# Other weights for spreading attention steps along the expert blocks

## The chip, the cores and the metric

The kernel runs on one core of one Trainium2 chip, as one launch. The metric is the device time in microseconds (us) of that launch. TensorE (PE) multiplies matrices, VectorE (DVE) and ScalarE (ACT) work on whole tiles, GpSimd (POOL) issues the indirect DMAs, SyncE (SP) issues the other DMAs.

## The reference

Two layers follow each other. The first is an attention over channels, for four batches of 5056 tokens by 256 channels. The second sends each of the 20224 token rows to one of eight experts, each with two matrices (256x1024 and 1024x256).

```python
qn = q / (norm(q, axis=1) + 1e-6); kn = k / (norm(k, axis=1) + 1e-6)
a  = softmax(kn.transpose(0, 2, 1) @ qn / tau)      # 256 x 256 in each batch
x  = (v @ a).reshape(B * N, 256)
e  = argmax(x @ w_gate, axis=1)                     # one expert for each row
out = gate_w * (relu(x @ w1[e]) @ w2[e])            # gate_w: the softmax weight of e
```

## The kernel before

**Side work and blocks.** A batch b has its attention cut into steps. For b = 2 and 3, 20 *chunks* of q and k give the scores (L205, L206); for b = 1 the scores come in the opening. 20 *norm* pieces give the column norms of the next batch (load L1268, square on ACT L1274). Then comes the *softmax*, and ten *groups* g = 0 to 9 of 512 tokens. A group takes: the values' scale (L1118, L1122), their two half-precision parts on ACT and DVE (L168, L175), four score products x t = 0 to 3 on PE (px, L1142), a copy of each from PSUM by ACT (xg, L1148), a square for the row's scale (xjunk, L1154), the choice of the expert on DVE (L388 to L412, r_m to r_ex), the *rank* products on PE (rtp, L417 and L420), the slots (L445, L448), the rows' two parts (L364 on ACT, L368 on DVE), and four scatters to DRAM by POOL (xs, L456).

The expert work is cut into 90 *blocks*: 72 of 256 rows and 18 of 128 rows, sorted by expert. A block n takes eight weight pieces that DVE copies out of the resident weights (wp, L629, five buffers), four first products on PE (hp, L640), a relu on ACT (L648) and the rest on DVE (ht, L651), four second products (y, L664), a scaling on ACT (o, L678) and two stores by POOL (out, L682). A first or a second product is a string of 12 matmuls. Strings of first products of block n and of second products of block n-1 alternate on PE.

**Stages.** A block can be loaded only when its rows have been scattered. Eleven places in the list of groups, ENDS, close a stage: (0,5), (0,9), and (b,2), (b,6), (b,9) for b = 1, 2, 3. After the rank of such a group a *table* is made: one product (ctp, L515) and some 27 small DVE operations (L518 to L578), from which the blocks of the next stage are known.

**The order.** PE, ACT, DVE and SP have their whole order written by a planner (lay, task). Each task has an engine, a guessed cost, what it depends on, and a due time; of the tasks that could start first on an engine the one with the earliest due time is taken. POOL takes its DMAs as they come. Once the order is made it is fixed: at run time an engine that waits holds all that is queued behind it.

**Due times of side work.** The list of side work, from group (0,8) on, is laid along the blocks: each entry has a weight, `amount` is the sum of the weights ahead of it, and an outline (hull) over the points (first block of a stage less two, amount at the stage's end) turns an amount into a block number. So an entry's due time follows from the weights alone, and the space that an entry gets is its weight's share. PE takes 10.48 us for a block of 256 rows with nothing else (1036.7 to 1047.2 in the trace).

Of the kernel before, what the change touches and what calls it, by code (L numbers as in the profile page):

```python
# [21 lines left out]
B, N, C = 4, 5056, 256  # L22
# [7 lines left out]
T = 4  # L30
# [4 lines left out]
ENDS = [(0, CUT - 1), (0, G - 1)] + [(b, g) for b in range(1, B) for g in (2, 6, G - 1)]  # L35
# [33 lines left out]
def attention_then_experts(ctx, tc, qk, qkc, vT, wts_in, kc, out):  # L69
# [33 lines left out]
    def halves(i):  # L103
        up = i % 2 == 0
        e = i // 2 if up else E - 1 - i // 2
        return e, ((2 * e, 2 * e + 1) if up else (2 * e + 1, 2 * e))
# [846 lines left out]
    for i in range(E):  # L953
        for k in range(2):
            task(("gram", i, k), pe, 0.93, [(("w", i, k), 1)] + ([("most", i - 1)] if i else []), call(w_gram, i, k), 5)
            n = halves(i)[1][k]
# [22 lines left out]
    for b in range(B):  # L979
        side = []  # L980
        if b == 1:
            side += [(("norm", b, n), 0.0, 0.6) for n in range(20)]
        if b > 1:
            side += [(("chunk", b, ch), 1.31, 1.2) for ch in range(NCH)]
        if b:
            side += [(("soft", b), 3.0, 7.0)]
        for g in range(AHEAD if b == 0 else 0, G):
            side += [(("x", b, g, t), 0.68 if b else 0.89, 1.9 if b else 1.2) for t in range(T)] + [(("rank", b, g), 0.3, 0.5)]
        for what, cost, weight in side:
            amount[what] = total  # L990
            total += weight
            done_by.append(total)
            spent.append(spent[-1] + cost)
            if what[0] == "rank" and what[1:] in ENDS[1:]:
                bounds.append(total)
# [473 lines left out]
```

## Time and profile before

| what | value |
|---|---|
| median of 3 runs | 1175.9 us (1173.66 to 1176.03) |
| the profiled execution | 1175.05 us |
| its span, first to last instruction | 1173.3 us |
| PE idle before 130 us (the opening) | 7.1 us |
| PE idle from 234 to 420 us (groups of b = 1) | 11.4 us |
| PE idle from 500 to 680 us (groups of b = 2) | 5.4 us |
| PE idle from 780 to 1000 us (groups of b = 3) | 2.3 us |

The opening (norms, scores of b = 0 and 1, the weights' scaling) lasts until 140.5 us, where block 0 starts. Blocks with side work follow until about 980 us, then blocks alone. An idle time in brackets behind a row of the time line is that of the engine just before the row, with what ended it; "issue" stands where the profile shows nothing that ended it.

### The profile page before, as it was taken

What the parts mean: (1) busy time and instruction counts of PE and PEld (TensorE: products, weight loads), DVE (VectorE), ACT (ScalarE), POOL (GpSimd) and SP (SyncE); (2) the same over time, 40 slices, a digit from 0 to 9 for tenths busy, and PEclk for the clock granted to TensorE, in tenths of its full rate; (3) what the DMA queues carried; (4) which work ended last, traced back from release to release, by engine and by line L of the source; (5) the groups of instructions that cost most, each with busy time, mean ns of one, the idle gap of its engine ahead of it and who ended that gap; (6) DMA issues with size and microseconds to landing.
All of it is one profiled execution on the core that took longest, in us unless ns stands there. A gap on an engine that the chain in (4) does not pass through costs nothing.

```text
span 1173.3 us, 28744 instructions
## 1 busy us (share of the span) xinstructions
PE 1136.9 (97%) x10325; PEld 992.6 (85%) x10325; DVE 903.8 (77%) x2624; ACT 673.2 (57%) x1475; POOL 358.8 (31%) x335
## 2 busy tenths in 40 slices
PE   9989999989999999999999999999999999999998
PEld 8878778878888777988878877888888888889997
DVE  5797676877778887787768797778788677767886
ACT  5575476577876555477776655466565443332332
POOL 0044432234343411143344321133343323322222
PEclk9999899999999999999999999999999999999999
DMA  9999679256764576255585366343342323322221
GB/s 368 408 405 333 170 232 258 79 166 179 201 183 112 131 201 178 56 154 145 172 217 156 103 187 190 83 101 96 97 115 67 73 55 61 79 60 48 45 47 35
DMA packets 155938, 177.40 MB, mean 151 GB/s; under 512 B 116972, under 2 KB 117233, under 8 KB 155792
## 3 DMA queue, kind: packets, MB, share of 16 engines
q1 hardware_dynamic: 139968, 132.74, 41.2%
q0 software_dynamic: 15824, 42.79, 10.7%
q8 instruction: 82, 1.34, 0.5%
q14 instruction: 64, 0.52, 0.1%
HBM read 111.48 MB, written 43.29 MB: 132 GB/s over the span
## 4 chain that ended last, share of the span: by engine, by line
PE 73%; issue 9%; DMA 7%; DVE 4%; ACT 3%; POOL 2%; another core or an unknown queue 1%; SPq 0%; POOLq 0%; DVEq 0%; ACTq 0%
PE hp L640 29%; PE y L664 29%; PE px L1142 6%; DMA raw<-in_qk 4%; DMA W<-in_w 3%; PE sp L205 3%; POOL out L682 2%; PE sp L183 2%; PE px L1054 2%; PE sp L206 1%; DVE hl L175 1%; ACT nraw L1274 1%; DVE ht L651 1%; DVE wp L629 1%
## 5 line engine op out<-in xcount | busy, mean ns | idle before, releaser
L640 PE MATMUL hp<-xT,wp 128*128 128x256 f16 (+1 forms) x4320 | 487.4, 263 | 9.2 <-issue 6.7
L664 PE MATMUL y<-wp,ht 128*128 128x256 f16 x3888 | 484.2, 273 | 7.9 <-issue 7.3
L640 PEld LDWEIGHTS <-wp 128*128 128x128 f16 x4320 | 390.6, 98 | 58.6 <-issue 10.8
L664 PEld LDWEIGHTS <-ht 128*128 128x128 f16 x3888 | 375.4, 98 | 56.2 <-issue 11.3
L629 DVE COPY wp<-W 128x1024 f16 x720 | 301.6, 436 | 118.3 <-PE hp L640 65.3
L648 ACT ACTIVATE ht<-hp 128x512 f16<-128x512 f32 x324 | 191.6, 593 | 274.2 <-PE hp L640 206.8
L682 POOL DMA_INDIRECT out<-o,mt x162 | 169.8, 1048 | 501.4 <-ACT o L678 462.3
L456 POOL DMA_INDIRECT xs<-rows,r_si x160 | 183.0, 1144 | 303.4 <-ACT W L143 69.7
L651 DVE SCALAR_TENSOR_TENSOR ht<-hp,ht 128x512 f16<-128x512 f32 x324 | 221.9, 685 | 49.6 <-ACT ht L648 41.4
L678 ACT ACTIVATE o<-y,b_fac 128x256 f32<-128x256 f32 x162 | 69.2, 469 | 53.8 <-PE y L664 25.0
L1142 PE MATMUL px<-a_h,hl 128*128 128x264 f16 x480 | 99.1, 276 | 0.4 <-DVE hl L175 0.3
L1142 PEld LDWEIGHTS <-hl 128*128 128x128 f16 x720 | 68.2, 98 | 12.3 <-issue 1.2
L168 ACT ACTIVATE hl<-raw,qk_s 128x512 f16<-128x512 f32 x80 | 53.3, 713 | 32.8 <-PE sp L206 25.1
L1148 ACT COPY xg<-px 128x264 f32<-128x264 f32 x128 | 47.5, 374 | 41.4 <-PE px L1142 14.2
L175 DVE SCALAR_TENSOR_TENSOR hl<-raw,qk_s,hl 128x512 f16<-128x512 f32 x80 | 56.2, 744 | 17.2 <-ACT hl L168 17.0
L1274 ACT ACTIVATE nraw<-nraw 128x1024 f32<-128x1024 f32 x60 | 63.1, 1052 | 6.9 <-DMA nraw<-in_qkc 5.0
L1142 PE MATMUL px<-a_l,hl 128*128 128x264 f16 x240 | 66.2, 276 | 0.2 <-issue 0.2
L364 ACT ACTIVATE rows<-xg,x_sc 128x256 f16<-128x256 f32 x128 | 56.0, 498 | 18.0 <-DVE x_sc L89 16.4
L1154 ACT ACTIVATE xjunk<-xg 128x256 bf16<-128x256 f32 x128 | 53.2, 416 | 3.0
L368 DVE SCALAR_TENSOR_TENSOR rows<-xg,x_sc,rows 128x256 f16<-128x256 f32 x128 | 54.3, 476 | 0.3 <-ACT rows L364 0.3
L205 PE MATMUL sp<-hl 128*128 128x512 f16 x160 | 54.2, 379 | 0.0
L206 PE MATMUL sp<-hl 128*128 128x256 f16 x160 | 43.6, 273 | 0.1
(186 smaller groups left out, 910.2 us busy)
## 6 DMA issues: line engine op xcount, KB each, us to landing
raw<-in_qk SPq DMA_DIRECT2D x80, 512.0 KB
nraw<-in_qkc SPq DMA_DIRECT2D x60, 512.0 KB
vraw<-in_vT SPq DMA_DIRECT2D x32, 512.0 KB
W<-in_w SPq DMA_DIRECT2D x28, 512.0 KB
v<-in_vT SPq DMA_DIRECT2D x16, 256.0 KB
out<-o,mt POOLq DMA_INDIRECT x162
xs<-rows,r_si POOLq DMA_INDIRECT x160
wraw<-in_w SPq DMA_DIRECT2D x4, 512.0 KB
```

Of the source, the lines that this page charges most:

```text
L175: vec.scalar_tensor_tensor(out=hl[:, 1, :, part], in0=raw[:, :, part], scalar=sc, in1=hl[:, 0, :, part], op0=ALU.mult, op1=ALU.subtract)
L205: pe.matmul(sp[c], hl[:, 0, j, kc0 : kc0 + P], hl[:, :, j, 0:C], start=first, stop=False)
L456: ins = pool.indirect_dma_start(out=xs[:, :], out_offset=bass.IndirectOffsetOnAxis(ap=si[:n, t : t + 1], axis=0), in_=rows[:n, t, :], in_o ...
L629: vec.tensor_copy(out=wps[n], in_=Wf[:, ds(b["e"] * 8192 + n * 1024, 1024)])
L640: pe.matmul(hps[f // nf][:, f % nf, :], wp[:, dc, wh, (f % 2) * P : (f % 2 + 1) * P], xT[:, 2 * xh + dc, :], start=(n == 0), stop=(n == 5),)
L648: act.activation(hts[h][:, 0], hps[h], AF.Relu)
L651: vec.scalar_tensor_tensor(out=hts[h][:, 1], in0=hps.pop(h), scalar=0.0, in1=hts[h][:, 0], op0=ALU.max, op1=ALU.subtract)
L664: pe.matmul(ys[j], hts[f // nf][:, hh, f % nf, j * P : (j + 1) * P], wp[:, f % 2, wh, :], start=(f == 0 and j == 0 and n == 0), stop=(f == ...
L678: act.activation(b["o", j], ys[j], AF.Copy, scale=b["fac"][:, j : j + 1])
L682: pool.indirect_dma_start(out=out[:, :], out_offset=bass.IndirectOffsetOnAxis(ap=load()[1].bitcast(I32)[:, j, 1:2], axis=0), in_=b.pop(("o ...
L1142: pe.matmul(pt, hl[:, vh, c, ts], ah[:, c, :], start=(n == 0), stop=(n == 5))
L1274: act.activation(raw, raw, AF.Square, accum_out=sums[b][:, n // 5, n % 5 : n % 5 + 1])
```

## The change

Only the weights are changed. A norm piece of b = 1 has 0.72 in place of 0.6, a softmax 10 in place of 7. A tile x has 2.0 for groups 3 to 7 of b = 1 and 2 (those beside which the next batch's norm pieces run), 1.5 for the other groups of b = 1 to 3, and 1.2 as before for b = 0; it was 1.9. A rank has 5.0 where the group closes a stage and 0.2 elsewhere; it was 0.5.

```diff
-            side += [(("norm", b, n), 0.0, 0.6) for n in range(20)]
+            side += [(("norm", b, n), 0.0, 0.72) for n in range(20)]
...
-            side += [(("soft", b), 3.0, 7.0)]
+            side += [(("soft", b), 3.0, 10.0)]
         for g in range(AHEAD if b == 0 else 0, G):
-            side += [(("x", b, g, t), 0.68 if b else 0.89, 1.9 if b else 1.2) for t in range(T)] + [(("rank", b, g), 0.3, 0.5)]
+            heavy = 2.0 if 0 < b < B - 1 and 3 <= g < 8 else 1.5 if b else 1.2
+            side += [(("x", b, g, t), 0.68 if b else 0.89, heavy) for t in range(T)]
+            side += [(("rank", b, g), 0.3, 5.0 if (b, g) in ENDS else 0.2)]
```

No operation is added or taken away; the same instructions stand in another order. A group of four tiles and a rank had 8.1 and has 8.2 (groups 3 to 7 of b = 1 and 2, or 13.0 with a stage's end), 6.2 or 11.0. Lines behind L980 have moved by two.

The first place is ACT at group (1,2), at block 9, about 253 to 262 us. Before, from a relu ahead of the copy of tile 2 (L1148) to the exponents of the choice (L1075):

```order
L648 ACTIVATE ht<-hp 128x512
L1148 COPY xg<-px 128x264
L168 ACTIVATE hl<-vraw,v_s 128x1024
L1154 ACTIVATE xjunk,x_ss<-xg 128x256
L1148 COPY xg<-px 128x264
L1154 ACTIVATE xjunk,x_ss<-xg 128x256
L1274 ACTIVATE nraw,n_sums<-nraw 128x1024
L648 ACTIVATE ht<-hp 128x512
L1075 ACTIVATE r_d<-r_d,v_s 128x32
```

And now:

```order
L648 ACTIVATE ht<-hp 128x512
L1150 COPY xg<-px 128x264 x2
L1156 ACTIVATE xjunk,x_ss<-xg 128x256 x2
L168 ACTIVATE hl<-vraw,v_s 128x1024
L1077 ACTIVATE r_d<-r_d,v_s 128x32
```

The last copy (tile 3) stood behind the values' upper part (L168) and a square; now it follows the copy of tile 2 at once, and the norm piece (L1274) has left the place.

The second place is DVE at the same group. Before, from a relu's rest to the count (L411, L412) that the rank product waits for:

```order
L651 SCALAR_TENSOR_TENSOR ht<-hp,ht 128x512
L629 ISA
L629 COPY wp<-W 128x1024
L175 SCALAR_TENSOR_TENSOR hl<-vraw,v_s,hl 128x1024
L388 TENSOR_REDUCE r_m<-xg 128x4
L390 TENSOR_TENSOR r_d<-xg,r_m 128x32
L392 SCALAR_TENSOR_TENSOR r_eq<-r_d,kt 128x32
L394 TENSOR_REDUCE r_r<-r_eq 128x4
L398 TENSOR_TENSOR r_oh<-kt,r_r 128x32
L411 TENSOR_TENSOR r_ex<-r_ex,r_oh 128x8 x3
L412 TENSOR_TENSOR r_ex<-r_ex,r_oh 128x8
```

And now:

```order
L651 SCALAR_TENSOR_TENSOR ht<-hp,ht 128x512
L388 TENSOR_REDUCE r_m<-xg 128x4
L390 TENSOR_TENSOR r_d<-xg,r_m 128x32
L392 SCALAR_TENSOR_TENSOR r_eq<-r_d,kt 128x32
L394 TENSOR_REDUCE r_r<-r_eq 128x4
L398 TENSOR_TENSOR r_oh<-kt,r_r 128x32
L411 TENSOR_TENSOR r_ex<-r_ex,r_oh 128x8 x3
L412 TENSOR_TENSOR r_ex<-r_ex,r_oh 128x8
L89 TENSOR_SCALAR x_sc<-x_ss 128x4
L629 ISA
L629 COPY wp<-W 128x1024
L175 SCALAR_TENSOR_TENSOR hl<-vraw,v_s,hl 128x1024
```

The weight copy and the values' lower part (L175) stood ahead of the choice and now stand behind the count.

The third place is ACT at group (1,7), at block 16, about 353 to 359 us. Before:

```order
L1148 COPY xg<-px 128x264
L1154 ACTIVATE xjunk,x_ss<-xg 128x256
L1118 ACTIVATE vjunk,v_b<-vraw 128x1024
L648 ACTIVATE ht<-hp 128x512
L168 ACTIVATE hl<-vraw,v_s 128x1024
L648 ACTIVATE ht<-hp 128x512
L1075 ACTIVATE r_d<-r_d,v_s 128x32
```

And now:

```order
L1120 ACTIVATE vjunk,v_b<-vraw 128x1024
L648 ACTIVATE ht<-hp 128x512
L168 ACTIVATE hl<-vraw,v_s 128x1024
L678 ACTIVATE o<-y,b_fac 128x256 x2
L648 ACTIVATE ht<-hp 128x512
L1150 COPY xg<-px 128x264
L1156 ACTIVATE xjunk,x_ss<-xg 128x256
L1077 ACTIVATE r_d<-r_d,v_s 128x32
```

The copy of tile 3 stood ahead of the next group's values (L1118, L168) and now comes after them, nearer to the choice; the values' parts are made earlier relative to it.

## The prediction

> **What bounds the kernel.** I read the page first, for the busy shares, then the windows, for where PE is idle, then PE's waits, then the time line around the longest of them.
>
> ```profile
> span 1173.3 us, 28744 instructions
> PE 1136.9 (97%) x10325; PEld 992.6 (85%) x10325; DVE 903.8 (77%) x2624; ACT 673.2 (57%) x1475; POOL 358.8 (31%) x335
> 130.00:1068.00 938.00, 914.32 (x8140) 791.92 (x8139) 721.93 (x2203) 566.67 (x1321) 303.61 (x287) 1.00 0.51 135
> 1068.00:1173.30 105.30, 99.67 (x1335) 93.95 (x1333) 82.98 (x197) 30.79 (x56) 23.14 (x21) 0.99 0.21 45
> ```
>
> The columns of a window are its length and then the busy time of PE, PE's weight loads, DVE, ACT and POOL. PE is the bound: idle for 36.4 of 1173.3 us. Of these, 23.7 lie between 130 and 1068 us, 5.6 behind (the last scaling and store, after PE's last product) and the rest in the opening. PE's work is the same in both orders, and the granted clock (last column but two) is 1.00 and 0.99. So the change can only move the 23.7 us. It could give at most 2.0%.
>
> ```profile
> 234.00:420.00 186.00, 174.63 (x1558) 149.44 (x1556) 148.75 (x505) 132.05 (x327) 71.12 (x66) 1.00 0.60 165
> 420.00:500.00 80.00, 80.00 (x682) 66.44 (x681) 59.87 (x134) 42.59 (x81) 10.77 (x10) 1.00 0.50 136
> 500.00:680.00 180.00, 174.62 (x1591) 152.64 (x1589) 143.34 (x486) 130.44 (x323) 71.91 (x67) 1.00 0.59 161
> 780.00:1000.00 220.00, 217.66 (x2004) 193.52 (x2002) 168.78 (x538) 118.19 (x293) 81.97 (x76) 1.00 0.33 81
> ```
>
> The loss sits in the groups of b = 1 (11.4 us) and b = 2 (5.4 us), where norm pieces load ACT to 71% and DVE to 80%. The chunks and the softmax of b = 2 (420 to 500 us) lose nothing, so the wider space of a softmax can give nothing by itself.
>
> ```profile
> PE y L664 <- issue: 7.3, 13, 1.1
> PE hp L640 <- issue: 6.7, 11, 1.1
> PE hp L640 <- DVE wp L629: 2.3, 3, 1.2
> PE rtp L420 <- DVE r_ex L411: 1.7, 5, 0.4
> PE rtp L417 <- DVE r_oh L398: 1.2, 1, 1.2
> ```
>
> These rows (total, times, longest) name three terms: rank products that wait for the choice, products that wait for DVE's weight copies, and 14.0 us in which PE waits for nothing that is shown.
>
> **Term 1, the rank waits.** A rank product holds every block string queued behind it on PE. The worst one is group (1,2):
>
> ```profile
> 253.81 1.16 ACT L168 ACTIVATE hl<-vraw,v_s 128x1024 f16<-128x1024 f32 x1
> 258.40 0.38 ACT L1148 COPY xg<-px 128x264 f32<-128x264 f32 x1 [3.03 <-remote]
> 258.66 1.27 DVE L175 SCALAR_TENSOR_TENSOR hl<-vraw,v_s,hl 128x1024 f16<-128x1024 f32 x1
> 259.86 0.17 DVE L388 TENSOR_REDUCE r_m<-xg 128x4 f32<-128x32 f32 x1
> 260.98 0.18 PE L417 MATMUL rtp<-r_oh,tri 128*128 128x32 f16 x1 [1.22 <-DVE r_oh L398]
> 261.58 0.18 PE L420 MATMUL rtp<-r_ex,ones 128*128 128x32 f16 x1 [0.42 <-DVE r_ex L411]
> ```
>
> The last tile's copy stood behind the 1.16 us upper part on ACT, and the choice behind the 1.27 us lower part on DVE. The orders shown above take both away, 2.4 us against waits of 1.22 + 0.42 = 1.64. I keep 0.3 of it, because a part of the delay, ACT's 3.03 us behind an unnamed releaser, is none of the order's.
>
> ```profile
> 320.15 0.18 PE L417 MATMUL rtp<-r_oh,tri 128*128 128x32 f16 x1 [0.30 <-DVE r_r L394]
> 320.73 0.18 PE L420 MATMUL rtp<-r_ex,ones 128*128 128x32 f16 x1 [0.41 <-DVE r_ex L411]
> 338.34 0.18 PE L420 MATMUL rtp<-r_ex,ones 128*128 128x32 f16 x1 [0.19 <-DVE r_ex L411]
> 340.78 0.17 PE L515 MATMUL ctp<-r_ex,ones 128*128 128x8 f16 x1 [0.27 <-DVE r_sl L445]
> 578.08 0.18 PE L420 MATMUL rtp<-r_ex,ones 128*128 128x32 f16 x1 [0.41 <-DVE r_ex L411]
> 597.93 0.18 PE L420 MATMUL rtp<-r_ex,ones 128*128 128x32 f16 x1 [0.31 <-DVE r_ex L411]
> 243.52 1.47 PE L664 MATMUL y<-wp,ht 128*128 128x256 f16 x12
> 244.83 1.47 PE L640 MATMUL hp<-xT,wp 128*128 128x256 f16 x12
> ```
>
> These are groups (1,5) with 0.71, (1,6) with 0.46 (its table's product included), (2,4) with 0.41 and (2,5) with 0.31; with (1,2), 3.53 in all. A string takes 1.31 us (the last two rows, start to start). Counting the strings and tiles that stand on PE between a group's last tile and its rank gives the cover of the choice. It grows from 4.6 to 5.9 us at (1,5), from 3.9 to 7.9 at (1,6), from 4.6 to 5.9 at (2,5) and from 5.2 to 9.2 at (2,6): these waits go. It shrinks to 3.9 us at (1,3), (2,4) and (2,7), each from 5.2, and at (1,7), from 7.2. There a wait may open; since the lower part now stands off the choice's path in most of them I leave 0.5 us for all four. So 3.53 becomes about 0.8: **-2.7 us**, between -3.5 and +4.1 (worked out below).
>
> **Term 2, the weight copies.**
>
> ```profile
> 250.24 1.48 PE L640 MATMUL hp<-xT,wp 128*128 128x256 f16 x12 [1.22 <-DVE wp L629]
> 359.81 0.40 PE L1142 MATMUL px<-a_h,hl 128*128 128x264 f16 x2 [0.32 <-DVE hl L175]
> 360.90 1.47 PE L664 MATMUL y<-wp,ht 128*128 128x256 f16 x12 [0.43 <-DVE wp L629]
> 409.79 1.48 PE L640 MATMUL hp<-xT,wp 128*128 128x256 f16 x12 [0.89 <-DVE wp L629]
> L651 DVE SCALAR_TENSOR_TENSOR ht<-hp,ht 128x512 f16<-128x512 f32 x324 | 221.9, 685 | 49.6 <-ACT ht L648 41.4
> ```
>
> At 250 us the order now has the weight copies together and ahead of a relu's rest (L651, 0.69 us on average) and three small operations; I take 0.7 of the 1.22. At 360 us, in block 16, the norm pieces and the next group's parts come earlier, so the 0.75 goes. At 409 us the table of stage 4 stands in one piece with the chunks' lower parts behind it, where before they were mixed: the same DVE work beside the same PE work, so I leave the 0.89 and the third wait of the row above (0.2). 0.7 + 0.75 is **-1.4 us**, between -3.1 (all) and +1.8 (a table in one piece delays copies at the two closing groups (1,9) and (2,9) by another 0.9 each, the price of the row at 409 us).
>
> **Term 3, the unnamed 14.0 us.** They are not spread evenly. They follow times when POOL issues six indirect DMAs without a break, four scatters and two stores. Here are the end of the first such run and of the last, the 20th, each with PE's wait:
>
> ```profile
> 171.00 1.04 POOL L682 DMA_INDIRECT out<-o,mt  x1 [0.30 <-issue]
> 171.78 0.38 PE L640 MATMUL hp<-xT,wp 128*128 128x256 f16 x2 [1.15 <-issue]
> ...
> 985.63 0.90 POOL L456 DMA_INDIRECT xs<-rows,r_si  x1 [0.30 <-issue]
> 986.83 0.99 POOL L682 DMA_INDIRECT out<-o,mt  x1 [0.30 <-issue]
> 987.71 0.61 PE L664 MATMUL y<-wp,ht 128*128 128x256 f16 x4 [0.45 <-issue]
> ```
>
> Stores come when a block ends, scatters some 4 us after a rank. By the distance on PE from a rank to the next block's end, such runs become one more in each of b = 1, 2 and 3. At 14.0 us for 20 runs, 0.7 each, that is +2.1. It is a coincidence in time, not a shown cause: so between 0 and 2.1, and I take **+0.9**. The Trainium skill, "SBUF — State Buffer", section "Who interferes with whom", says that TensorE has ports of its own and waits for no one, and that DMA never contends with a compute engine. By that rule the runs of six hold nobody and the term is 0; the rows above are against it, as far as a coincidence goes.
>
> **Other edits.** The norm pieces of b = 1 have more space, in blocks 1 to 5, where PE's only waits are of the unnamed kind, as at 171 us: nothing taken. SP's loads of values and norm pieces move with their users; among PE's waits behind 140 us none names a load, so PE's cover over them is whole; a load that came a tile late would hold ACT first and show as a longer rank wait. The last table comes two blocks earlier, but the blocks alone behind it lose nothing: no gain.
>
> **Sum.** -2.7 - 1.4 + 0.9 = -3.2 us. From the profiled execution's own 1175.05 (0.85 under the median of the three runs, 1175.9) that gives **1171.8 us**.
>
> **The rivals.**
> *The rank waits move (slower).* The four groups whose cover shrinks to 3.9 us are ones with norm pieces on ACT. What their chain takes, from the last tile to the count, is seen at (2,4) before:
>
> ```profile
> 572.13 0.28 PE L1142 MATMUL px<-a_h,hl 128*128 128x264 f16 x1
> 575.03 0.36 ACT L1148 COPY xg<-px 128x264 f32<-128x264 f32 x1
> 578.06 0.16 DVE L412 TENSOR_TENSOR r_ex<-r_ex,r_oh 128x8 f16<-128x8 f16 x1
> ```
>
> From 572.41 to 578.22 it is 5.8 us. If the chain stays so, each of the four waits 1.9 us: +7.6, less the 3.5 that goes elsewhere, +4.1 for term 1 in place of -2.7. With terms 2 and 3 as above that is +3.6, 1178.6. It decides where ACT hands over the copy later than about 2 us after the tile. For it speaks that ACT works as much in these groups as before (a norm piece for each tile); against it that the 1.27 us lower part is no longer in front.
>
> *Given back (no change).* DVE is busy for 148.75 of the 186 us of b = 1, in bunches where it is late for several users. A wait saved at one place is then waited at the next, as the 1.22 us at 250 us and the 1.64 at 261 us may be one backlog. If half of the gain in terms 1 and 2 is given back and term 3 costs its 2.1: -4.1/2 + 2.1 = 0, 1175.1.
>
> *The unnamed waits shrink too.* They lie in the same crowded stretches. If the spread takes away half of the 14.0 us instead of adding 0.9, the sum is -4.1 - 7.0, 1163.9.
>
> **Chances.** The forecast 0.47, moved waits 0.18, given back 0.22, unnamed waits 0.13. The range takes in the first three and the nearer part of the last: 1165 to 1179. A measurement tells about 0.2% (2.4 us) from no change. Against 1175.9, the forecast is faster by more in some 0.40 of its 0.47, and the last case always: 0.52 with what is left of small changes at 0.29 and slower at 0.19.
>
> **What would show it.** In the changed profile: the rank rows at groups (1,2), (1,5), (1,6) and (2,5) without a wait of over 0.3 us; no weight copy wait over 0.4 us near 250 and 360 us; PE's idle time from 234 to 420 us down from 11.4 to some 8 us, and 420 to 500 us still at zero. Rank waits of over 1 us at (1,3), (1,7), (2,4) or (2,7) would show the slower rival; an "issue" sum well away from 14 to 16 us would show that term 3 was not what I took it for. A fall of the granted clock, or a block that waits for its load, would make the sum wrong altogether.

## The result

| | median | range | runs |
|---|---|---|---|
| before | 1175.7 us | 1172.85 to 1176.53 | 6 |
| after | 1185.7 us | 1182.97 to 1187.43 | 6 |

The changed kernel takes 1.0088 of the time before (95% interval 1.0069 to 1.0107): some 10 us slower, where 1171.8 us was forecast and 1179 was the upper end. The profiled execution of after took 1182.97 us, 7.9 more than that of before.

In two of the five sets of runs below the kernel before took about 1151 us instead of 1176, and the traces of those sets show next to none (0.4 us at most) of the unnamed waits of the third term; each ratio is therefore taken within its set, and the sets are called *with* and *without unnamed waits*.

The page of after and its windows, the latter with the same columns as before:

```profile
span 1181.3 us, 28724 instructions
PE 1137.4 (96%) x10325; PEld 991.4 (84%) x10325; DVE 905.7 (77%) x2624; ACT 676.0 (57%) x1475; POOL 358.7 (30%) x335
130.00:1078.00 948.00, 916.95 (x8167) 792.46 (x8167) 724.39 (x2204) 569.06 (x1320) 305.04 (x287) 1.00 0.49 134
```

PE's work is what it was (1137.4 against 1136.9 us); its idle time between the opening and the end of the side work is 31.1 us (948.00 - 916.95) against 23.7. That is 7.4 of the 8.0 us by which the span grew. PE's waits in the profile of after (total, times, longest):

```profile
PE y L664 <- issue: 7.3, 14, 1.1
PE px L1144 <- issue: 4.6, 7, 1.3
PE hp L640 <- DVE wp L629: 4.2, 4, 1.5
PE hp L640 <- issue: 3.5, 6, 0.8
PE ctp L515 <- DVE r_sl L445: 2.0, 3, 0.9
PE rtp L420 <- DVE r_ex L411: 1.7, 4, 0.4
PE rtp L417 <- DVE r_oh L398: 1.3, 2, 0.9
PE y L664 <- DVE c_tb L578: 1.1, 1, 1.1
PE px L1144 <- DVE hl L175: 1.1, 3, 0.4
PE y L664 <- DVE wp L629: 0.9, 2, 0.6
PE rtp L417 <- DVE v_s L89: 0.6, 1, 0.6
PE hp L640 <- DVE c_sf L562: 0.3, 1, 0.3
```

Put together by kind and set against before: waits for weight copies and for what stands with the tables (wp, ctp, c_tb, c_sf) 8.5 us against 3.0 (2.3 and 0.4 for copies, and the 0.27 of the table's product); rank products 3.6 against 3.2; the lower part hl 1.1 against 0.3; unnamed 15.4 in the first, second and fourth row against 14.0. The first kind is the large one.

Now by place. These are the sums of ten windows of 24 us, each from 4 us ahead of the rank of a group that closes a stage ((0,9), then (b,2), (b,6), (b,9)), first of before and then of after (window lengths, then PE, PEld, DVE, ACT, POOL; then means):

```profile
sum 240.00, PE 228.41 PEld 196.03 DVE 206.02 ACT 160.08 POOL 81.65; mean PE 22.84 PEld 19.60 DVE 20.60 ACT 16.01 POOL 8.17
```

```profile
sum 240.00, PE 220.90 PEld 189.01 DVE 194.92 ACT 139.81 POOL 85.19; mean PE 22.09 PEld 18.90 DVE 19.49 ACT 13.98 POOL 8.52
```

PE is idle for 11.6 us in them before and for 19.1 after: +7.5. In the rest of the stretch from 130 us to the end of the side work (1068 and 1078 us) it is 12.1 us before (23.7 - 11.6) and 12.0 after. So the loss lies where a stage closes, which is where the rank's new weight of 5.0 acts. It is not spread over all ten. At four of them, (2,2), (2,6), (3,2) and (3,6), PE is idle for 8.0 us against 0.6 before, and 6.7 of the 8.0 are unnamed. Here is (3,2), before and after:

```profile
809.00:833.00 24.00, 24.00 (x225) 21.42 (x224) 21.73 (x87) 16.88 (x42) 9.01 (x8) 1.00 0.37 90
```

```profile
809.00:833.00 24.00, 21.17 (x191) 17.93 (x189) 19.42 (x72) 14.29 (x34) 8.34 (x8) 1.00 0.25 72
```

At the other six it is 11.1 us against 11.0, but of another kind: copies and tables have 5.4 of it where they had 1.2, and ranks and unnamed waits have as much less. So the unnamed waits grew little in all, but they moved to other places.

What happens at one of the six is seen at group (1,2), where the rank wait itself is gone as forecast (rows from the time line of after, PE and DVE):

```profile
256.28 0.38 PE L664 MATMUL y<-wp,ht 128*128 128x256 f16 x2 [1.13 <-issue]
256.42 0.43 DVE L629 COPY wp<-W 128x1024 f16 x1 [1.97 <-remote]
...
256.53 0.18 PE L420 MATMUL rtp<-r_ex,ones 128*128 128x32 f16 x1
256.55 1.47 PE L640 MATMUL hp<-xT,wp 128*128 128x256 f16 x12
256.77 1.28 DVE L175 SCALAR_TENSOR_TENSOR hl<-vraw,v_s,hl 128x1024 f16<-128x1024 f32 x1
...
258.72 0.18 DVE L445 TENSOR_TENSOR r_sl<-rtp,r_oh 128x32 f32<-128x32 f32 x1
258.96 0.17 PE L515 MATMUL ctp<-r_ex,ones 128*128 128x8 f16 x1 [0.94 <-DVE r_sl L445]
...
267.96 0.15 DVE L578 TENSOR_SCALAR c_tb<-c_sf 1x6 int32<-1x6 f32 x1
268.04 0.41 DVE L629 COPY wp<-W 128x1024 f16 x1
268.85 1.36 PE L664 MATMUL y<-wp,ht 128*128 128x256 f16 x11 [1.13 <-DVE c_tb L578]
```

The table's product (L515) now stands a single string behind the rank, and waits for the slots (L445), which stand on DVE behind the lower part (L175) and four small operations. Ten us later a string waits 1.13 us, by the profile for the table's last operation (L578); the copy behind it ends at 268.45. The 1.64 us that the rank lost here before come back as 2.1 in two other waits. Ahead of them stands a delay that the profile can't explain: PE was idle for 1.13 us, and the copy ahead of the lower part came on DVE after 1.97 us of idle time ("remote" is a releaser that the profile doesn't know).

### The profile page after: what moved, and what is told of

Same layout as the page of the kernel before. It is cut to its first block, busy times and chain, and to the rows that moved or that the text cites. A ratio compares the mean times of both kernels' runs of the same rounds, so it can differ in the third digit from the quotient of the medians.

```text
span 1181.3 us, 28724 instructions
## 1 busy us (share of the span) xinstructions
PE 1137.4 (96%) x10325; PEld 991.4 (84%) x10325; DVE 905.7 (77%) x2624; ACT 676.0 (57%) x1475; POOL 358.7 (30%) x335
## 4 chain that ended last, share of the span: by engine, by line
PE 70%; issue 9%; DVE 8%; DMA 7%; ACT 3%; POOL 2%; another core or an unknown queue 1%; DVEq 0%; POOLq 0%; SPq 0%; ACTq 0%
PE hp L640 27%; PE y L664 27%; PE px L1144 6%; DMA raw<-in_qk 3%; PE sp L205 3%; DMA W<-in_w 2%; POOL out L682 2%; PE sp L183 2%; DVE wp L629 2%; PE sp L206 2%; PE px L1056 2%; DVE ht L651 1%; DVE hl L175 1%; DVE rows L368 1%; DMA v<-in_vT 1%
## 5 line engine op out<-in xcount | busy, mean ns | idle before, releaser
L456 POOL DMA_INDIRECT xs<-rows,r_si x160 | 184.1, 1151 | 315.9 <-ACT W L143 69.4
L168 ACT ACTIVATE hl<-raw,qk_s 128x512 f16<-128x512 f32 x80 | 53.4, 715 | 41.4 <-PE sp L206 37.6
L175 DVE SCALAR_TENSOR_TENSOR hl<-raw,qk_s,hl 128x512 f16<-128x512 f32 x80 | 56.4, 748 | 19.1 <-ACT hl L168 18.9
```

What stands on the lines that cost most here:

```text
L175: vec.scalar_tensor_tensor(out=hl[:, 1, :, part], in0=raw[:, :, part], scalar=sc, in1=hl[:, 0, :, part], op0=ALU.mult, op1=ALU.subtract)
L456: ins = pool.indirect_dma_start(out=xs[:, :], out_offset=bass.IndirectOffsetOnAxis(ap=si[:n, t : t + 1], axis=0), in_=rows[:n, t, :], in_o ...
```

## The experiments

**1. Each edit alone.**

```diff
rank_only, on before:
-    ... + [(("rank", b, g), 0.3, 0.5)]
+    ... + [(("rank", b, g), 0.3, 5.0 if (b, g) in ENDS else 0.2)]
x_only, on before:
-    (("x", b, g, t), ..., 1.9 if b else 1.2)
+    (("x", b, g, t), ..., 2.0 if 0 < b < B - 1 and 3 <= g < 8 else 1.5 if b else 1.2)
soft_only, on before:
-    (("soft", b), 3.0, 7.0)
+    (("soft", b), 3.0, 10.0)
norm_only, on before:
-    (("norm", b, n), 0.0, 0.6)
+    (("norm", b, n), 0.0, 0.72)
```

> Theory A (the rank's weight at a stage's end costs the time: it draws the groups ahead of a stage's end together, puts the table's product close behind its rank on PE and its 27 small DVE operations in one piece ahead of weight copies): +8 to +10 us against before, with table product waits (L515) of 2 us in all and weight copy waits of 4 us or more. Theory B (the lighter tiles of x cost it): within 3 us of before. Theory C (softmax and norms): within 3 us of before.

> Theory B (tiles of x with 1.5 in place of 1.9 stand denser on the blocks, most of all in b = 3, where PE's idle time rose from 2.3 to 6.9 us): +5 to +10 us, with the rise in b = 3 seen again. Theory A (the rank's weight): within 3 us of before, b = 3 as before.

> Theory C (the softmax's wider space takes it from the groups): +4 us or more, spread over the groups of b = 1, 2 and 3. Theories A and B, and the prediction: within 2.4 us of before.

> Theory C in its other half (norm pieces of b = 1 later, so that the groups of b = 1 have less): +2 us or more, all of it in b = 1. Theories A and B, and the prediction: within 2.4 us of before.

| kernel (before 1176.4 us) | time, us | of before | 95% interval |
|---|---|---|---|
| rank_only | 1193.7 | 1.0137 | 1.0101 to 1.0174 |
| x_only | 1176.7 | 0.9998 | 0.9981 to 1.0015 |
| soft_only | 1178.8 | 1.0029 | 1.0008 to 1.0049 |
| norm_only | 1177.5 | 1.0019 | 1.0006 to 1.0033 |

The rank's weights cost more alone (16 us by the ratio, and more than theory A had given them) than the whole change does; the tiles of x cost nothing, the softmax 3 us and the norm 2. In the profile of the kernel with only the rank's weights:

```profile
PE y L664 <- issue: 14.1, 22, 1.4
PE hp L640 <- DVE wp L629: 6.6, 9, 1.5
PE px L1142 <- issue: 4.1, 5, 1.1
PE hp L640 <- issue: 3.4, 8, 1.0
PE ctp L515 <- DVE r_sl L445: 2.2, 2, 1.2
```

Product waits of 2 us and copy waits over 4 were theory A's signs, and both are there. They are not the whole cost: the unnamed waits are 21.6 us against 14.0 before. Nor does the time follow the named waits alone, since the kernel with only the tiles of x has 7.0 us of waits for copies and tables in its profile and 11.4 of unnamed ones, at the time of before. The edits don't add up (16 + 3 + 2 against 10): with the lighter tiles of x the same 5.0 is laid over other blocks.

**2. What of the rank's weight.** It does two things: it squeezes all groups (by the weights' shares the four tiles of a group of b = 1 or 2 have 1.37 blocks before and 1.23 with only the rank's weights), since its 5.0 lies behind the rank and no side work stands there (theory A1 below); and it draws the closing rank with its table forward against the blocks' due times (theory A2).

```diff
after_rank_old, on after:
-            side += [(("rank", b, g), 0.3, 5.0 if (b, g) in ENDS else 0.2)]
+            side += [(("rank", b, g), 0.3, 0.5)]
closing_tiles, on before:
-    (("x", b, g, t), ..., 1.9 if b else 1.2)
+    (("x", b, g, t), ..., 3.025 if b and (b, g) in ENDS else 1.9 if b else 1.2)
rank_table_later, on rank_only (and after_table_later on after, before_table_later on before):
-            when = 2 if b == 0 and g < AHEAD else due(("rank", b, g)) + 2
+            when = 2 if b == 0 and g < AHEAD else due(("rank", b, g)) + 7
```

> After with the rank's weight back at 0.5 for all groups; the other weights stay as changed. Theory A (the rank's weight costs the time): 1175 to 1179 us, 7 us or more under after. Rival (several weights cost it together, and the rank's 16 us alone are a thing of the old tiles of 1.9): 1182 us or more.

> Before, with the 4.5 that the changed rank adds at a stage's end laid on the four tiles of the closing group (3.025 each) and 0.5 on every rank. The other groups are squeezed as in the kernel with only the rank's weights (1.23 blocks each against 1.37), but the closing group has more space and its rank is at the stage's end. Theory A1 (the squeeze of the groups costs it): 1187 us or more. Theory A2 (the closing rank and its table being drawn forward costs it): 1174 to 1180 us.

> The kernel with only the rank's weights, with a table's due time 5 us later (7 behind the rank's in place of 2). Theory A2 (the table's product and its burst on DVE close behind the rank cost it): 4 us or more below 1191 us, and no table product wait (L515) over 0.4 us. Theory A1 (the squeeze): within 3 us of 1191.

This set was one without unnamed waits. Of before (1150.5 us here) after_rank_old took 1.0007 (0.9994 to 1.0021), closing_tiles 1.0039 (1.0028 to 1.0050), rank_table_later 0.9990 (0.9976 to 1.0005). By ratio, theory A's expectation of after_rank_old holds: without the rank's weight the change costs nothing in this set. But neither after nor rank_only was run in it, so what the weight costs there isn't shown. Squeezing the groups as much, but with the rank at the stage's end, cost 4.5 us, between what the two theories gave it. As the set differed from the first, the decisive pair was run again on one chip, with after and its own version.

> The kernel with only the rank's weights again, beside the next three on one chip, since the earlier chips differed (before took 1176.4 us on the first, 1150.5 us on the second, whose traces show none of the unnamed issue waits). If the cost of the rank's weights is a matter of the order alone: 1.010 to 1.017 of before on any chip. If it comes through the unnamed waits: under 1.006 on a chip without them, 1.010 or more on a chip with them.

> Only the rank's weights, tables due 5 us later; it took 0.999 of before on the second chip. Theory A2 (the table close behind its rank costs it): within 0.4% of before on this chip too, and at least 8 us under the run with only the rank's weights. Rival (the chip made the difference): within 3 us of the run with only the rank's weights.

> After as it is, on the chip of the others. Order alone: 1.007 to 1.011 of before on any chip. Through the unnamed waits: under 1.005 on a chip without them.

> After with tables due 5 us later. Theory A2: 7 us or more under after, no table product wait (L515) over 0.4 us and no weight copy wait behind a table over 1 us. Theory A1 (the squeeze of the groups): within 3 us of after.

| kernel (set with unnamed waits) | time, us | of before | 95% interval |
|---|---|---|---|
| rank_only_b | 1197.3 | 1.0193 | 1.0162 to 1.0225 |
| rank_table_later_b | 1176.7 | 1.0007 | 0.9991 to 1.0024 |
| after_b | 1187.4 | 1.0093 | 1.0061 to 1.0124 |
| after_table_later | 1176.4 | 1.0004 | 0.9990 to 1.0018 |

Both costs are there again (that of rank_only_b is above the 1.017 that was expected at most). Five microseconds in one due time, with the squeeze left as it is, take back all of the cost: 20.6 us in the one pair and 11.0 in the other. Theory A2 holds and A1 falls. The windows around the ten stage ends and the waits of after_table_later:

```profile
sum 240.00, PE 227.48 PEld 193.92 DVE 193.09 ACT 143.49 POOL 91.37; mean PE 22.75 PEld 19.39 DVE 19.31 ACT 14.35 POOL 9.14
```

```profile
PE hp L640 <- DVE wp L629: 1.7, 2, 1.2
PE y L664 <- DVE wp L629: 1.2, 2, 0.9
PE y L664 <- DVE c_ni L518: 0.6, 1, 0.6
```

The idle time there is 12.5 us, near to the 11.6 of before. No table product waits, and copies and tables stand at 3.5 us where after had 8.5. What comes back comes back at the six ends named above, where PE's idle time is 5.9 us against 12.5 in after_b. At the other four it stays at 6.6 us against 7.0, and 6.0 of it are unnamed: that part does not hang on the table's due time.

**3. Product or burst.** A table has two parts: its product on PE, and some 27 small operations on DVE. Between the first and the last of these before had three to five weight copies at each of the ten later stages; after has none at (2,2), (2,6), (3,2) and (3,6). Yet behind these four no copy or product wait follows in after, after_b or after_c. The waits for products and copies stand mainly at (1,2), (1,9) and (2,9), where a table still has four copies inside.

```diff
after_pace2, on after:
-                table_tasks(st, (b, g), when, 1.0 if st else 0.0)
+                table_tasks(st, (b, g), when, 2.0 if st else 0.0)
before_table_early, on before:
-            when = 2 if b == 0 and g < AHEAD else due(("rank", b, g)) + 2
+            when = 2 if b == 0 and g < AHEAD else due(("rank", b, g)) - 1
...
-                table_tasks(st, (b, g), when, 1.0 if st else 0.0)
+                table_tasks(st, (b, g), when, 0.2 if st else 0.0)
```

> After with a table's DVE steps due 2 us apart in place of 1; the strings on PE between a rank and its table's product are the same as in after. Theory burst (small DVE operations in one piece hold weight copies): 5 us or more under after (1.0091 of before), so under 1.005 of before. Theory product (the table's product behind the slots): within 2.4 us of after, 1.007 to 1.011.

> Before with tables due 3 us earlier and their DVE steps 0.2 us apart, so that the tables of all ten later stages stand in one piece, with no weight copy and nothing else among their operations. Weights as before. Theory burst: four such tables went with 10 us in after, so ten make 1.015 or more of before. Rival (the groups that the weights squeeze cost it, and a table in one piece only beside squeezed groups): within 3 us of before.

> Before with tables due 5 us later. By the burst theory the weight copies within tables fall from 42 to 28 in ten tables here, but none is in one piece, so little is left to gain: 0.995 to 1.000 of before. Rival (blocks then wait for their tables): 1.003 or more, with PE waiting for a block's load.

A set without unnamed waits again (before 1151.2 us). after_pace2 took 0.9993 of before (0.9978 to 1.0008), before_table_early 1.0191 (1.0147 to 1.0234), before_table_later 1.0004 (0.9985 to 1.0023). Tables in one piece, and due 3 us earlier, cost 21 us with the old weights and no squeeze at all. Here is the longest wait of that kernel, with the table at (1,6), PE and DVE:

```profile
334.18 0.43 DVE L629 COPY wp<-W 128x1024 f16 x1
...
336.07 0.15 DVE L518 SCALAR_TENSOR_TENSOR c_ni<-ctp,kt 1x8 int32<-1x8 f32 x1
336.15 1.47 PE L640 MATMUL hp<-xT,wp 128*128 128x256 f16 x12
...
340.51 0.16 DVE L578 TENSOR_SCALAR c_tb<-c_sf 1x8 int32<-1x8 f32 x1
340.59 0.86 DVE L368 SCALAR_TENSOR_TENSOR rows<-xg,x_sc,rows 128x256 f16<-128x256 f32 x2
341.39 0.41 DVE L629 COPY wp<-W 128x1024 f16 x1
...
341.85 2.68 PE L664 MATMUL y<-wp,ht 128*128 128x256 f16 x12 [4.22 <-DVE wp L629]
```

From 334.6 to 341.4 us DVE makes no weight copy, 4.6 of it for operations on at most 64 numbers, and PE, which takes a piece every 1.31 us, runs dry for 4.22 us. Only two copies lie between this stretch and one of 6.4 us ahead of it, so the ring of five buffers can't have been full. Its copy waits are 15.7 us in all, it has no product wait, and its clock falls four times (the last section; some 7 us by the price given there):

```profile
PE y L664 <- DVE wp L629: 10.2, 4, 4.2
PE hp L640 <- DVE wp L629: 5.5, 4, 1.9
```

So a burst can by itself cost as much as was seen, but in after the tables in one piece are not where such waits stand. after_pace2, which leaves the table's product as close behind its rank as after has it, shows no product wait and loses nothing. At (1,2) its order on DVE and PE from the choice to the table's product is that of after:

```profile
257.36 0.17 PE L515 MATMUL ctp<-r_ex,ones 128*128 128x8 f16 x1
```

PE is not idle ahead of it, and there is no unnamed wait at this place, so the 0.94 us there in after came behind the unnamed delay. But after itself was never run in a set without unnamed waits. How its own cost divides between product, burst and unnamed delays that a table close behind its rank hands on, and whether it would lose anything without them, stays open. Tables due later on the kernel before gain nothing: its tables were loose already. No version that does the whole work is faster than before by more than its interval.

**4. The unnamed waits.**

```diff
no_store, on before (no_store_b and no_store_c are the same):
-            task(("store", n, j), pool, 1.15, [("result", n, j)], call(store, j), d(15) + 5, ...)
+            task(("store", n, j), pool, 1.15, [("result", n, j)], call(store, j) if st == LAST else lambda: None, d(15) + 5, ...)
```

> Before without the stores of the 72 blocks of 256 rows (the output's rows of those blocks stay unwritten); PE, ACT, DVE and SP keep their order. The prediction's term 3 (runs of six indirect DMAs on POOL hold PE): the unnamed issue waits behind 130 us fall from 14.0 to under 3 us, and the time to about 1164. Rival (the runs of six only fall together with crowded stretches): 12 to 16 us of such waits stay, and the time is within 3 us of before.

> Before without the stores of the 72 blocks of 256 rows. On a chip whose other kernels of this call show the unnamed issue waits: term 3's coincidence being a cause, under 3 us of them are left behind 130 us and the time is 0.985 to 0.990 of before; not a cause: 10 us or more of them are left. On a chip without such waits: 0.995 again, and nothing is told.

> After as it is. Where the traces of this call show the unnamed issue waits: 1.007 to 1.011 of before once more. Where they do not: the four tables in one piece cost weight copy waits (before_table_early had 15.7 us of them with ten such tables, so some 6 us here), 1.004 to 1.007 of before; by the rival (the change costs only through the unnamed waits) under 1.002.

> Before without the stores of the 72 blocks of 256 rows. Where the traces of this call show the unnamed issue waits, and the runs of six being their cause: under 3 us of them behind 130 us, 0.985 to 0.990 of before. Not their cause: 10 us or more of them. Where they do not show them: 0.995 to 0.997 of before, and nothing is told.

This kernel leaves out the stores of the 72 blocks of 256 rows. The first two runs fell into sets without such waits and told nothing of them (0.9949, interval 0.9934 to 0.9963, and 0.9963, interval 0.9944 to 0.9982). The third set had them: after_c took 1186.1 us, 1.0085 of before (1.0064 to 1.0105), and no_store_c 1149.2, 0.9775 (0.9752 to 0.9798). The unnamed rows of after_c and then the one of no_store_c:

```profile
PE y L664 <- issue: 7.6, 12, 1.2
PE hp L640 <- issue: 4.8, 9, 0.8
PE px L1144 <- issue: 3.7, 5, 1.1
```

```profile
PE y L664 <- issue: 0.3, 1, 0.3
```

Without the stores the unnamed waits are gone, and so are the rank waits but for 0.4 us. The stores are thus part of their cause. The gain is twice what was expected (0.985 to 0.990): the waits in the rows of before are only 14 us of it, and PE's busy time, for the same matmuls, is 1128.2 us against 1136.9, so another part of the cost doesn't show as a wait.

The sum of these waits also goes with the number of runs of six or more indirect DMAs behind 130 us with no longer break than 0.4 us: 17 runs and 11.4 us in x_only, 19 and 14.0 in before, 22 and 15.4 in after, 25 and 21.6 in rank_only. The runs are not the whole cause, since in the sets without these waits POOL issues them in the same way (20 in after_rank_old) and PE does not stop.

## Why the prediction was wrong

**What bounds the kernel** was right: PE's work is unchanged, and only the idle time of 130 to 1068 us moved. It was taken that the softmax and chunk stretch has nothing to give, and from 420 to 500 us PE is idle for none of it in both kernels.

**Term 1 (forecast -2.7, measured +0.4)** was right where it looked. No rank product at (1,2), (1,5), (1,6) or (2,5) waits for over 0.3 us any more, and none at (1,3), (1,7), (2,4) or (2,7): the slower rival's mechanism did not come. But new rank waits opened where nothing was counted, at groups whose tiles became lighter (1.5): 1.31 us at (1,8), and 0.41 to 0.78 at (2,8), (3,2), (3,4) and (3,5). Only groups that waited before, and four of b = 1 and 2 whose cover shrinks, had been looked at. (The prediction counted the table's product in term 1 and the lower part in term 2. Sorted like that, term 1 measured +2.1 and term 2 +4.6; the sum is the same.)

**Term 2 (forecast -1.4, bound +1.8, measured +5.5)** is the step that failed. The 0.75 us at block 16 went down to 0.25, but the copy wait at 250 us stayed (1.17 us at 248.17). The price of a table was seen and then left at the bound: as a matter of two closing groups, (1,9) and (2,9), at 0.9 us each, from one wait of the trace before. The sentence "the same DVE work beside the same PE work, so I leave the 0.89" held at its own place, (1,9), where 0.39 and 0.27 us are waited now. At (2,9), where before had none, it came to 2.19 (0.67 for the product, and 1.52 behind the chunks' lower parts), and at (1,2), which no bound counted, to 2.07. Another 1.26 us stand behind (1,5), which closes no stage. That the rank's weight moves the table at every closing group, close behind its rank, was the step left out, and the runs with a later table show that it is what the time hangs on.

**Term 3 (forecast +0.9, measured +1.4)** had the right size. The runs of six became three more, as forecast, though one came in b = 1 and two in b = 3; counted with no break over 0.4 us there were 19 before, not 20. What was only a coincidence is now borne out in part. The rule of the Trainium skill, "SBUF — State Buffer", section "Who interferes with whom", by which TensorE waits for no one, would have left the unnamed waits where they were without the stores; they fell to 0.3 us, where the other kernels of the sets with such waits have 11 us or more. What it is that holds PE was not found, nor whether SBUF's ports, which that section is about, have a part in it.

**Other edits** were taken at nothing. The tiles of x are that (0.9998), but the softmax and the norm pieces, alone, cost some 0.3 and 0.2%.

**Sum.** -3.2 us were forecast and +7.9 measured between the two profiled executions: about 5.5 from copies and tables, 0.4 from ranks, 0.8 from lower parts and 1.4 from unnamed waits (some of the first may be delays handed on from the last, as at (1,2)). The medians differ by 2 us more, since the profiled execution of after is its shortest; part of the others is the clock, below.

Of the rivals "given back" came nearest in kind: what the rank saved at (1,2) was waited for again 2 and 12 us later. It was priced at no change, and the way back cost more than the gain.

## What to carry to other kernels

When weights or due times move a step, follow everything that hangs on it to the engine that feeds the bound one: here the time hung not on the rank but on the table behind it, one product and 27 small operations among the copies that TensorE lives on. A ring of buffers covers a stretch of the feeding engine's other work no longer than its pieces last, and the length of the stretch doesn't tell alone: 6.8 us without a copy cost 4.22 us at (1,6) of before_table_early, close behind another such stretch, and no copy wait at (2,6) of after. Count the copies inside and ahead of each such stretch in both orders before calling the work the same. And try the suspected step's due time by itself: five microseconds there told more than all the weights. Then look at the waits by kind and by place together: here the sums by kind and the places of the loss point at different waits.

## What was not expected of the hardware

**The clock falls after a stretch that is half idle.** Two windows of after_b, one behind the other:

```profile
545.89:549.30 3.41, 1.70 (x13) 0.99 (x12) 1.49 (x4) 2.11 (x5) 1.09 (x2) 1.00 0.22 77
549.30:552.71 3.41, 3.41 (x18) 2.43 (x17) 1.83 (x5) 1.64 (x6) 0.00 (x0) 0.50 0.79 191
```

PE was busy for 1.70 of 3.41 us, with no idle piece of over 0.92, and ran at half its clock for the next 3.41, in which it did 18 matmuls, where the 3.41 us ahead of these windows had 33. The twenty profiles of this case have 21 such falls between 150 and 1100 us, and in the 3.41 us ahead of each PE was idle for 1.70 us or more. Not every stretch with as much is followed by a fall (after was idle for 2.05 us between 901.3 and 904.7 us, and its clock stayed at 1.00), so it may count where the stretch begins; that was not tested. A fall costs some 1.7 us (half of 3.41), and a few small waits close together are enough; executions of after range from 1183 to 1187 us, at mean granted clocks of 0.999 to 0.996. The Trainium skill, "TensorE: Matmul & The Clock Gate", section "What's actually happening", has windows of about 3.4 us and a fall after an idle one; the length agrees, but here a window that is half idle was enough.

**The unnamed waits stop several engines and come and go by the set of runs.** At the stage end (3,6) of after, POOL's last issues of a run of six, PE and ACT:

```profile
899.94 0.99 POOL L682 DMA_INDIRECT out<-o,mt  x1 [0.30 <-issue]
901.23 0.99 POOL L682 DMA_INDIRECT out<-o,mt  x1 [0.30 <-issue]
902.02 0.27 PE L1144 MATMUL px<-a_h,hl 128*128 128x264 f16 x1 [0.71 <-issue]
903.74 0.39 PE L1144 MATMUL px<-a_h,hl 128*128 128x264 f16 x2 [1.33 <-issue]
903.81 1.09 ACT L648 ACTIVATE ht<-hp 128x512 f16<-128x512 f32 x2 [5.21 <-remote]
```

PE stops in the middle of one product of x, and ACT's relu starts 2.5 us after its string has ended (899.83 + 1.47). The same chip gave before in 1176 us in one set and in 1151 in another, so it is not a property of a chip. What differs between the sets was not found.
